# A mixture of experts in slots: slots sorted by size on the chip, short ones run over 256 columns, token numbers loaded two slots ahead

## The chip, the cores and the metric

The kernel runs on one core of a Trainium2 chip. The metric is the device time of one execution in microseconds. Engines are named as in the profile: PE is TensorE (PEld its weight loads), DVE is VectorE, ACT is ScalarE, POOL is GpSimd, SP is SyncE. A DMA is issued by the queue of one of SP, ACT or POOL; `SPq`, `ACTq` and `POOLq` are those sequencers.

## The reference

Three stages follow each other, on 4608 tokens of width 512.

```python
# attention without a softmax over pairs, 8 batches x 8 heads x 576 x 64
q_s = softmax(q, axis=-1); k_s = softmax(k, axis=2)
x = einsum('bhsd,bhde->bhse', q_s, einsum('bhsd,bhse->bhde', k_s, v))   # -> x[4608, 512]
# mixture of 8 experts, each token goes to one
logits = x @ w_gate + modality_bias[modality_id]
e_idx = argmax(logits, axis=1); gate_w = softmax(logits)[arange(N), e_idx]
for e in range(8):
    mask = e_idx == e
    out[mask] = gate_w[mask, None] * (maximum(x[mask] @ w1[e], 0) @ w2[e])   # 512 -> 1024 -> 512
# a dense layer: 512 -> 2048 -> 512, leaky relu
g = maximum(0.01 * (out @ w_in), out @ w_in);  result = g @ w_out
```

The two weight matrices of the dense layer are of type float64.

## The kernel before

Attention and router run first (`attention`), in four passes over pairs of batches. `phase_r` finds for each token its expert, its gate and its place, and scatters (token number, gate) with GpSimd's indirect DMAs into a DRAM table `region`, where each expert has 4608 rows (L384). Its tile `tg` holds the pairs to be scattered and has two buffers (L322).

`slot_tables` (L431 to L471) then works out, on the chip, how the tokens fall into slots of at most 512 rows of one expert, in the order of the experts, and leaves three integers per slot in `ti`: the expert, the first row in `region`, and the first column in `dense`. The number of slots used stands behind them. There are at most 16; slots 0 to 8 always run (`NSTATIC = 9`), slots 9 to 15 stand in nested `tc.If(ns > s)` (L692 to L699).

A slot (`slot`, L648) has two passes. Pass 1 makes 8 products of 12 matmuls over 512 columns each: a weight and an operand are each split in a high and a low part, and three of the four combinations are summed. Its result `hp` (three PSUM buffers) goes through ScalarE (`hh`, L566) and VectorE (`hl`, L567). Pass 2 makes 4 products of 24 matmuls, copied by ScalarE to `y` (L581, two buffers) and stored to `dense` by SyncE (L582). Between them stand, in the order of the code and so on each engine's queue:

- the splits of the weights for this slot's pass 2 (in pass 1) and of the next slot's pass 1 (in pass 2): `wsplit`, one ScalarE cast (L475) and one VectorE subtraction (L476) each, with the loads of weights from DRAM five pieces ahead in a ring of six buffers (L517, SyncE);
- for the next slot, `xload` at the slot's start: SyncE loads its token numbers and gates into `idt` (L541), VectorE makes integers `idi` of them (L543), GpSimd gathers the rows `xg` by four indirect DMAs (L545). After pass 1 ScalarE multiplies them by the gates (`xgate`, L551); in the second and third product of pass 2 TensorE transposes them (`xprep`, L556) and they are split into `xh` and `xl`;
- in slots 0 to 7 a conversion of the float64 weights, `f64` (L597 to L630): 16 pieces, two per slot, four steps each, of which one stands after every second product of pass 1 and one after each product of pass 2. Step 1 masks on VectorE (L610), clamps on GpSimd (L611) and loads the next piece; step 2 shifts (L615, L616); step 3 combines (L618, L619); step 4 makes four differences (L623) and splits them (`rh`, `rl`);
- in slot 8, loads for the dense layer (L748, L755).

```python
        w1 products:  for f in range(8): pass1(f); wsplit or step()
        if s + 1 < NSLOT:
            xgate(s + 1)
        for t in range(4):
            pass2(s, t, o, mid); wsplit(s + 1, 1, t); step()
```

[...] `Hidden.run` (L778) and `last_product` (L937) are the dense layer; their matmuls have 256 columns.

Of the kernel before, what the change touches and what calls it, by code (L numbers as in the profile page):

```python
# [93 lines left out]
def attention(ctx, tc, cst, a, region, xd):  # L94
# [208 lines left out]
    def phase_r(i, c0, c1):  # L303
# [122 lines left out]
SP = mybir.EngineType.SP  # L426
# [52 lines left out]
def experts(ctx, tc, cst, a, region, xd, dense, did, wops, pre):  # L479
# [17 lines left out]
    idts = [wp.tile([128, 4, 2], F32, name=f"idt{i}") for i in range(2)]  # L497
# [61 lines left out]
    def pass1(f):  # L559
# [6 lines left out]
        nc.scalar.activation(out=hh[:, f], in_=hp, func=AF.Relu)  # L566
        nc.vector.scalar_tensor_tensor(out=hl[:, f], in0=hp, scalar=0.0, in1=hh[:, f].bitcast(F32),  # L567
                                       op0=ALU.max, op1=ALU.subtract)

    def pass2(s, d, o, mid):  # L570
        yp = ps.tile([128, SLOT], F32, tag="y", name="yp")
        n = 0
        for f in range(8):
            for w, h in ((w2h, hh), (w2l, hh), (w2h, hl)):
                nc.tensor.matmul(yp, lhsT=w[:, f, 128 * d:128 * d + 128], rhs=h[:, f], start=(n == 0), stop=(n == 23))  # L575
                n += 1
# [4 lines left out]
        nc.scalar.copy(out=y, in_=yp)  # L581
        nc.sync.dma_start(out=dense[128 * d:128 * d + 128, bass.ds(o, SLOT)], in_=y)  # L582
# [14 lines left out]
    def f64(cv, name, i, w, ahead, behind):  # L597
# [13 lines left out]
        nc.gpsimd.tensor_scalar(out=t.bitcast(F32), in0=t.bitcast(F32), scalar1=CLAMP_LO, scalar2=CLAMP_HI, op0=ALU.max, op1=ALU.min)  # L611
# [36 lines left out]
    def slot(s, step=lambda: None, mid2=lambda t: None):  # L648
        if s + 1 < NSLOT:
            xload(s + 1)  # L650
        for f in range(8):
            pass1(f)
# [4 lines left out]
        if s + 1 < NSLOT:  # L657
# [3 lines left out]
                          in_=idts[s % 2].rearrange("p t c -> p (t c)"))  # L661
        for t in range(4):
# [5 lines left out]
            pass2(s, t, o, mid)  # L668
# [3 lines left out]

    loads_to(AHEAD)
# [417 lines left out]
```

## Time and profile before

| | us |
|---|---|
| runs | 1483.12, 1485.05, 1486.98 (median 1485.05) |
| profiled execution | 1477.94 |
| its span | 1476.2 |
| attention and router, to the first slot | 0 to 221 |
| ten slots | 221 to 720 |
| dense layer, first matrix | 723 to 1100 |
| dense layer, second matrix | 1105 to 1476 |
| TensorE busy | 1338.4 (91%) |
| VectorE, ScalarE, GpSimd busy | 1031.6, 600.5, 403.9 |
| mean granted clock of TensorE | 0.968 |

The profiled execution is 7 us shorter than the median of the runs. In the rows of a timeline the bracket at the end is the time that the engine was idle before the instruction, and what ended it. Matmuls are pipelined: of a run of matmuls the starts tell the pace, not the durations.

### The profile page before, as it was taken

To read this page: it belongs to the slowest core of one execution; us is meant where nothing else is said; L and a number is where in the kernel's file an instruction comes from. 1 tells how busy PE (TensorE), PEld (TensorE's weight loads), DVE (VectorE), ACT (ScalarE), POOL (GpSimd) and SP (SyncE) were. 2 spreads that over 40 slices of the span, in tenths; PEclk is the share of its full clock that TensorE was granted. 3 is DMA by queue.
4 is the path that set the end of the run, shared out by engine and by line. 5 is a ranking of instruction groups with operands and counts; after the bars stand their busy time and mean duration, and the time that the engine had idled before them with its cause. 6 is when DMAs were issued, how large, how long until landed. Compare 5 with 4: busy or idle time off the path is not lost.

```text
span 1476.2 us, 23214 instructions
## 1 busy us (share of the span) xinstructions
PE 1338.4 (91%) x9083; PEld 1229.8 (83%) x9083; DVE 1031.6 (70%) x1347; ACT 600.5 (41%) x946; POOL 403.9 (27%) x273
## 2 busy tenths in 40 slices
PE   4778718999999999989989999999989999999998
PEld 3668606777777777768889999999989999999998
DVE  5788626677767767634558777777767777777775
ACT  3566414555455545534423223332324333333332
POOL 2447532313231323011033434333331111101111
PEclk9899958999999999989999999999999999999999
DMA  9564245877787779565583333333297443443430
GB/s 374 205 241 154 103 133 171 260 242 233 249 274 232 232 246 305 194 221 179 184 346 144 121 137 136 122 133 125 103 417 295 143 143 117 135 133 118 143 115 30
DMA packets 144519, 280.05 MB, mean 190 GB/s; under 512 B 17808, under 2 KB 69520, under 8 KB 141456
## 3 DMA queue, kind: packets, MB, share of 16 engines
q1 hardware_dynamic: 125376, 218.94, 44.0%
q10 hardware_dynamic: 11472, 38.52, 6.4%
q0 software_dynamic: 7552, 21.02, 4.0%
q8 instruction: 74, 1.21, 0.3%
q14 instruction: 45, 0.37, 0.1%
HBM read 181.59 MB, written 96.85 MB: 189 GB/s over the span
## 4 chain that ended last, share of the span: by engine, by line
issue 26%; DVE 9%; PE 6%; POOL 6%; DMA 2%; ACT 1%; POOLq 0%; SPq 0%; DVEq 0%
PE hp L778 6%; POOL out L959 3%; POOL s L818 2%; DMA wi<-wid 2%; DVE ht L791 1%; DVE ht L824 1%; DVE ht L827 1%; DVE s L815 1%; DVE ht L811 1%; DVE s L813 1%; DVE x L476 1%; POOL s L819 1%; DVE xl L476 0%; ACT ht L820 0%; ACT xh L475 0%
## 5 line engine op out<-in xcount | busy, mean ns | idle before, releaser
L778 PE MATMUL hp<-xh,wi 128*128 128x256 f32 x1152 | 212.9, 281 | 3.7 <-DVE ht L827 2.3
L937 PE MATMUL yp<-wi,x 128*128 128x256 f32 x1152 | 191.5, 284 | 0.0
L778 PEld LDWEIGHTS hp<-xh,wi 128*128 128x128 f32 x1152 | 179.4, 188 | 6.3 <-DVE ht L827 3.8
L937 PE MATMUL yp<-wi,wi 128*128 128x256 f32 x1200 | 178.3, 283 | 0.3 <-DVE wi L476 0.3
L778 PE MATMUL hp<-x,wi 128*128 128x256 f32 x1296 | 166.7, 289 | 8.1 <-DMA wi<-wid 3.9
L778 PEld LDWEIGHTS hp<-x,wi 128*128 128x128 f32 x1296 | 163.1, 197 | 8.9 <-DVE ht L827 4.1
L937 PEld LDWEIGHTS yp<-wi,wi 128*128 128x128 f32 x1200 | 163.5, 192 | 0.5 <-DVE wi L476 0.5
L937 PEld LDWEIGHTS yp<-wi,x 128*128 128x128 f32 x1152 | 161.9, 192 | 0.1
L778 PE MATMUL hp<-xl,wi 128*128 128x256 f32 x576 | 160.8, 279 | 0.0
L564 PE MATMUL hp<-xh,w1h 128*128 128x512 f32 x320 | 129.7, 405 | 27.8 <-DVE hl L567 27.8
L959 POOL DMA_INDIRECT out<-yo,idx x36 | 47.4, 1317 | 314.9 <-DVE idx L953 294.3
L564 PE MATMUL hp<-xl,w1h 128*128 128x512 f32 x320 | 127.6, 399 | 0.0
L564 PE MATMUL hp<-xh,w1l 128*128 128x512 f32 x320 | 127.2, 397 | 0.0
L575 PE MATMUL yp<-hh,w2h 128*128 128x512 f32 x320 | 126.4, 395 | 0.0
L575 PE MATMUL yp<-hl,w2h 128*128 128x512 f32 x320 | 124.8, 390 | 0.0
L575 PE MATMUL yp<-hh,w2l 128*128 128x512 f32 x320 | 124.7, 390 | 0.0
L545 POOL DMA_INDIRECT xg<-xd,idi x44 | 58.3, 1325 | 237.5 <-DVE hl L567 216.8
L818 POOL TENSOR_TENSOR s<-s,s 128x512 f32<-128x512 f32 x36 | 48.3, 1343 | 226.4 <-DVE s L815 160.8
L778 PEld LDWEIGHTS hp<-xl,wi 128*128 128x128 f32 x576 | 108.0, 187 | 0.0
L791 DVE SCALAR_TENSOR_TENSOR ht<-ht 128x1024 f32<-128x1024 f32 x72 | 104.8, 1455 | 2.5
L476 DVE TENSOR_TENSOR w1l<-st,w1h 128x1024 fp32r<-128x1024 f32 x44 | 53.8, 1227 | 71.3 <-ACT w1h L475 71.3
L564 PEld LDWEIGHTS hp<-xh,w1h 128*128 128x128 f32 x320 | 61.9, 193 | 46.9 <-DVE hl L567 34.1
(202 smaller groups left out, 2629.4 us busy)
## 6 DMA issues: line engine op xcount, KB each, us to landing
st<-in_w SPq DMA_DIRECT2D x89, 512.0 KB, 5.1
hd<-ht ACTq DMA_DIRECT2D x72, 512.0 KB, 3.2
xt<-hd SPq DMA_DIRECT2D x18, 1024.0 KB, 5.4
hr<-hd SPq DMA_DIRECT2D x18, 1024.0 KB, 5.5
wi<-wid SPq DMA_DIRECT2D x28, 512.0 KB, 8.4
wi<-wod SPq DMA_DIRECT2D x6, 2048.0 KB, 13.2
v<-in_v SPq DMA_DIRECT2D x8, 1300.0 KB, 13.0
dense<-y SPq DMA_DIRECT2D x40, 256.0 KB, 3.3
```

The costliest lines, as they stand in the source:

```text
L476: nc.vector.tensor_tensor(out=lo, in0=src, in1=hi.bitcast(F32), op=ALU.subtract)
L545: nc.gpsimd.indirect_dma_start(out=xg[:, t], out_offset=None, in_=xd, in_offset=bass.IndirectOffsetOnAxis(ap=idi[:, t:t + 1], axis=0), bou ...
L564: nc.tensor.matmul(hp, lhsT=w[:, k, 128 * f:128 * f + 128], rhs=x[:, k], start=(n == 0), stop=(n == 11))
L575: nc.tensor.matmul(yp, lhsT=w[:, f, 128 * d:128 * d + 128], rhs=h[:, f], start=(n == 0), stop=(n == 23))
L778: self.nc.tensor.matmul(bank[:, g], lhsT=w[:, h, k, 128 * g:128 * g + 128], rhs=x[:, k], start=(n == 0), stop=(n == 5))
L791: V.scalar_tensor_tensor(out=c, in0=c, scalar=0.01, in1=c, op0=ALU.mult, op1=ALU.max)
L811: V.tensor_tensor(out=h[:, 0, 0], in0=bank, in1=s[1], op=ALU.add)
L813: V.tensor_tensor(out=s[6], in0=bank, in1=s[1], op=ALU.add)
L815: V.tensor_tensor(out=s[7], in0=bank, in1=s[6], op=ALU.add)
L818: G.tensor_tensor(out=s[6], in0=s[6], in1=s[5], op=ALU.add)
L937: nc.tensor.matmul(bank, lhsT=x[:, k], rhs=w[i][:, h, k], start=(c == 0), stop=(c == 23))
L959: ins = nc.gpsimd.indirect_dma_start(out=out, out_offset=bass.IndirectOffsetOnAxis(ap=idi[s % 2][:, t:t + 1], axis=0), in_=y[:, t], in_off ...
```

## The change

- **Slots sorted.** `slot_tables` counts for each expert the slots of more than 256 rows and those of up to 256, lays out all of the first kind and then all of the second (17 positions in place of 9, 16 sums in place of 8), and leaves behind the 48 integers the number of slots of the first kind (`nb`) and of all (`ns`).
- **Short slots.** In the seven dynamic blocks each slot is there twice, chosen by `tc.If(nb > s)`: as before, or with `rows=slice(0, 256)`, where matmuls, `hh`, `hl`, `y` and the store take 256 columns. The static slots stay wide.
- **Token numbers** of slot s + 2 are loaded in the middle of slot s (`idload`), into one of three buffers; those of slots 0 and 1 at the start, the first ahead of all weights.
- **Stores of `dense`** are issued by ScalarE in place of SyncE, so the column `o` is read into a register of ScalarE too.
- **The clamp** of the conversion is made by VectorE in place of GpSimd.
- `tg` has three buffers.

```diff
-            t["tg"] = sp.tile([128, NC, 2], F32, tag="tg", name="tg")
+            t["tg"] = sp.tile([128, NC, 2], F32, tag="tg", name="tg", bufs=3)
...
-    d = con.tile([128, 2, 9], F32, name="sd")
+    d = con.tile([128, 2, 17], F32, name="sd")
-    V.tensor_tensor(out=g, in0=bc(d[:, 1, 1:9], 2, 9), in1=bc(cst["k512"], 1, NE), op=ALU.is_gt)
-    V.tensor_reduce(out=d[:, 0, 1:9], in_=g, axis=AX.X, op=ALU.add)
+    V.tensor_tensor(out=g[:, 0], in0=bc(n[:, :], 2, 9), in1=bc(cst["k512"], 1, NE), op=ALU.is_gt)
+    V.scalar_tensor_tensor(out=g[:, 1], in0=bc(n[:, :], 2, 9), scalar=-256.0, in1=bc(cst["k512"], 1, NE), op0=ALU.add, op1=ALU.is_gt)
+    V.tensor_reduce(out=m, in_=g, axis=AX.X, op=ALU.add)
+    V.tensor_copy(out=d[:, 0, 1:9], in_=m[:, 1])
+    V.tensor_tensor(out=d[:, 0, 9:17], in0=m[:, 0], in1=m[:, 1], op=ALU.subtract)
...
     def reg(s, f, mx):
-        return nc.values_load(ti[0:1, 3 * s + f:3 * s + f + 1], engines=[SP], min_val=0, max_val=mx)
+        return nc.values_load(ti[0:1, 3 * s + f:3 * s + f + 1], engines=[SP] + [ACT] * (f == 2), min_val=0, max_val=mx)
...
+    def idload(s):
+        if s < NSLOT:
+            nc.sync.dma_start(out=idts[s % 3].rearrange("p t c -> p (t c)"),
+                              in_=region[bass.ds(reg(s, 1, NE * NT), SLOT), :].rearrange("(p t) c -> p (t c)", t=4))
+
     def xload(s):
-        r = reg(s, 1, NE * NT)
-        idt, idi = idts[s % 2], idis[s % 2]
-        nc.sync.dma_start(out=idt.rearrange("p t c -> p (t c)"),
-                          in_=region[bass.ds(r, SLOT), :].rearrange("(p t) c -> p (t c)", t=4))
+        idt, idi = idts[s % 3], idis[s % 2]
         nc.vector.tensor_copy(out=idi, in_=idt[:, :, 0])
...
-                nc.tensor.matmul(hp, lhsT=w[:, k, 128 * f:128 * f + 128], rhs=x[:, k], start=(n == 0), stop=(n == 11))
+                nc.tensor.matmul(hp[:, rows], lhsT=w[:, k, 128 * f:128 * f + 128], rhs=x[:, k, rows], start=(n == 0), stop=(n == 11))
...
-        nc.scalar.copy(out=y, in_=yp)
-        nc.sync.dma_start(out=dense[128 * d:128 * d + 128, bass.ds(o, SLOT)], in_=y)
+        nc.scalar.copy(out=y[:, rows], in_=yp[:, rows])
+        nc.scalar.dma_start(out=dense[128 * d:128 * d + 128, bass.ds(o, rows.stop)], in_=y[:, rows])
...
-        nc.gpsimd.tensor_scalar(out=t.bitcast(F32), in0=t.bitcast(F32), scalar1=CLAMP_LO, scalar2=CLAMP_HI, op0=ALU.max, op1=ALU.min)
+        V.tensor_scalar(out=t.bitcast(F32), in0=t.bitcast(F32), scalar1=CLAMP_LO, scalar2=CLAMP_HI, op0=ALU.max, op1=ALU.min)
...
         nc.sync.dma_start(out=did[bass.ds(o, SLOT)].rearrange("(p t) c -> p (t c)", t=4),
-                          in_=idts[s % 2].rearrange("p t c -> p (t c)"))
+                          in_=idts[s % 3].rearrange("p t c -> p (t c)"))
+        idload(s + 2)
...
+    idload(0)
+    loads_to(2)
+    idload(1)
     loads_to(AHEAD)
     xload(0)
...
-    ns = nc.values_load(ti[0:1, 3 * NSLOT:3 * NSLOT + 1], min_val=NSTATIC, max_val=NSLOT)
+    nb = nc.values_load(ti[0:1, 3 * NSLOT:3 * NSLOT + 1], min_val=0, max_val=NSLOT)
+    ns = nc.values_load(ti[0:1, 3 * NSLOT + 1:3 * NSLOT + 2], min_val=NSTATIC, max_val=NSLOT)
...
         with tc.If(ns > s):
-            slot(s)
+            before = dict(stage), list(cnt), nload[0]
+            regs.clear()
+            with tc.If(nb > s) as big:
+                slot(s)
...
+            with big.Else():
+                slot(s, rows=slice(0, SLOT // 2))
+            regs.clear()
             more(s + 1)
```

How it moves instructions shows at three places. SyncE's queue at the start of the slots, before (`st` is the ring of weights, `ti` the tables, L505 a register load):

```order
L517 DMA st_1857<-in_w 128x4x256
L517 ISA
L517 DMA st_1858<-in_w 128x4x256
L517 ISA
L517 DMA st_1859<-in_w 128x4x256
L517 ISA
L517 DMA st_1860<-in_w 128x2x512
L505 TENSOR_LOAD ti
L505 ISA x2
L541 ISA
L541 DMA idt_1862<-region 128x8
```

and now:

```order
L552 ISA
L552 DMA idt_1873<-region 128x8
L517 TENSOR_LOAD ti
L517 ISA x2
L529 ISA
L529 DMA st_1867<-in_w 128x4x256
L529 ISA
L529 DMA st_1868<-in_w 128x4x256
L517 TENSOR_LOAD ti
L517 ISA x2
L552 ISA
L552 DMA idt_1874<-region 128x8
```

The load of `idt` for slot 0 stood behind five loads of weights and now stands ahead of all of them; that of slot 1 stood after the first slot's pass 1 had begun and now follows two loads of weights.

ScalarE's queue at the end of a slot and the start of the next, before (`y` the copy of a product of pass 2, `rh` the conversion's split, `hh` the first product of pass 1):

```order
L581 COPY y_1868<-yp 128x512
L475 CAST w1h<-st_1859 128x4x256
L475 CAST xh<-tp 128x4x128 x2
L581 COPY y_1867<-yp 128x512
L475 CAST w1h<-st_1860 128x4x256
L581 COPY y_1868<-yp 128x512
L475 CAST w1h<-st_1861 128x4x256
L475 CAST rh<-r 128x1792
L566 ACTIVATE hh<-hp 128x512
```

and now:

```order
L595 COPY y_1879<-yp 128x512
L596 ISA
L596 DMA dense<-y_1879 128x512
L487 CAST w1h<-st_1869 128x4x256
L595 COPY y_1880<-yp 128x512
L596 ISA
L596 DMA dense<-y_1880 128x512
L487 CAST w1h<-st_1870 128x4x256
L487 CAST rh<-r 128x1792
L580 ACTIVATE hh<-hp 128x512
L487 CAST w2h<-st_1871 128x1024
L580 ACTIVATE hh<-hp 128x512 x2
```

Behind each copy stands the issue of its store, ahead of the next cast.

VectorE's queue in the same pass 1, before (`idi` the integers, `w2l` a split of weights):

```order
L476 TENSOR_TENSOR rl<-r,rh 128x1792
L543 CAST idi_1864<-idt_1862 128x4
L567 SCALAR_TENSOR_TENSOR hl<-hp,hh 128x512
L476 TENSOR_TENSOR w2l<-st_1856,w2h 128x1024
L567 SCALAR_TENSOR_TENSOR hl<-hp,hh 128x512
L610 TENSOR_SCALAR r<-w 128x1024
L567 SCALAR_TENSOR_TENSOR hl<-hp,hh 128x512
L476 TENSOR_TENSOR w2l<-st_1857,w2h 128x1024
L567 SCALAR_TENSOR_TENSOR hl<-hp,hh 128x512
L615 TENSOR_SCALAR w<-w 128x1024
L616 TENSOR_SCALAR r<-r 128x1024
L567 SCALAR_TENSOR_TENSOR hl<-hp,hh 128x512
```

and now:

```order
L488 TENSOR_TENSOR rl<-r,rh 128x1792
L557 CAST idi_1876<-idt_1875 128x4
L581 SCALAR_TENSOR_TENSOR hl<-hp,hh 128x512
L488 TENSOR_TENSOR w2l<-st_1867,w2h 128x1024
L581 SCALAR_TENSOR_TENSOR hl<-hp,hh 128x512
L624 TENSOR_SCALAR r<-w 128x1024
L625 TENSOR_SCALAR r<-r 128x1024
L581 SCALAR_TENSOR_TENSOR hl<-hp,hh 128x512
L488 TENSOR_TENSOR w2l<-st_1868,w2h 128x1024
L581 SCALAR_TENSOR_TENSOR hl<-hp,hh 128x512
L629 TENSOR_SCALAR w<-w 128x1024
L630 TENSOR_SCALAR r<-r 128x1024
```

The clamp (L625) stands right behind the mask; the shifts keep their places.

## Rows read from the trace of the kernel before

**Rows 1.** The page, part 1: busy time, share of the span, instructions.
```profile
PE 1338.4 (91%) x9083; PEld 1229.8 (83%) x9083; DVE 1031.6 (70%) x1347; ACT 600.5 (41%) x946; POOL 403.9 (27%) x273
```

**Rows 2.** Windows: slots 0, 1-7, 3, 8, 9; length, engines busy, clock, DMA share, GB/s.
```profile
221.20:275.90 54.70, 48.78 (x211) 39.93 (x210) 35.91 (x40) 25.43 (x32) 12.53 (x6) 0.91 0.60 189
275.90:616.20 340.30, 325.55 (x1458) 264.07 (x1457) 242.40 (x288) 168.71 (x210) 89.23 (x42) 0.99 0.78 250
373.20:422.30 49.10, 47.27 (x210) 38.77 (x209) 35.92 (x42) 24.08 (x30) 12.61 (x6) 0.97 0.77 243
616.20:674.30 58.10, 48.42 (x210) 39.62 (x209) 23.97 (x29) 23.66 (x31) 5.82 (x4) 0.91 0.66 216
674.30:720.00 45.70, 45.63 (x210) 37.60 (x208) 19.33 (x21) 21.14 (x28) 5.26 (x4) 1.00 0.47 147
```

**Rows 3.** Waits of PE (185 to 765) and ACT: total us, times, longest.
```profile
PE hp L564 <- DVE hl L567: 27.8, 15, 9.7
...
ACT y L581 <- DMA dense<-y: 28.5, 6, 5.6
```

**Rows 4.** Timeline, slot 8: start, us, engine, line, operation, [idle before, releaser].
```profile
627.28 0.36 SPq L541 DMA_DIRECT2D idt<-region  x1
...
633.53 0.17 DVE L543 CAST idi<-idt 128x4 int32<-128x4 f32 x1 [8.89 <-DMA idt<-region]
...
634.35 0.79 PE L564 MATMUL hp<-xh,w1h 128*128 128x512 f32 x1 [9.68 <-DVE hl L567]
```

**Rows 5.** Timeline of SP and DVE, from the tables to slot 0's pass 1.
```profile
196.67 2.92 SPq L517 DMA_DIRECT2D st<-in_w  x5
201.82 0.35 SPq L541 DMA_DIRECT2D idt<-region  x1
...
207.28 0.17 DVE L543 CAST idi<-idt 128x4 int32<-128x4 f32 x1 [11.64 <-DMA idt<-region]
...
226.75 1.02 SPq L594 DMA_DIRECT2D w<-in_win  x2
...
236.00 0.17 DVE L543 CAST idi<-idt 128x4 int32<-128x4 f32 x1 [8.65 <-DMA idt<-region]
```

**Rows 6.** Timeline, slot 1, pass 1 and the start of pass 2.
```profile
296.67 0.69 DVE L616 TENSOR_SCALAR r<-r 128x1024 int32<-128x1024 int32 x1 [4.59 <-POOL r L611]
...
298.02 0.50 PE L564 MATMUL hp<-xh,w1h 128*128 128x512 f32 x1 [0.39 <-DVE hl L567]
...
310.18 0.76 PE L556 MATMUL tp<-cf,xg 128*128 128x128 f32 x5 [0.28 <-ACT xg L551]
```

**Rows 7.** Timeline, end of slot 3 (SP, ACT) and start of slot 7 (PE).
```profile
411.13 3.13 SPq L594 DMA_DIRECT2D w<-in_wout  x2
...
424.32 0.59 ACT L581 COPY y<-yp 128x512 f32<-128x512 f32 x1 [5.59 <-DMA dense<-y]
...
577.48 0.50 PE L564 MATMUL hp<-xh,w1h 128*128 128x512 f32 x1 [0.81 <-DVE hl L567]
```

**Rows 8.** Window in the last product, L937 alone: length, PE and PEld busy, clock.
```profile
1200.00:1300.00 100.00, 100.00 (x837) 100.00 (x837) 1.00 0.42 132
```

**Rows 9.** Exit of the slots: timeline; L695, L690: durations ns min/median/max, first and last start.
```profile
721.79 0.55 SPq L517 DMA_DIRECT2D st<-in_w  x1
722.96 7.18 PE L778 MATMUL hp<-x,wi 128*128 128x256 f32 x36 [3.03 <-DVEq L695]
...
L695 SPq EVENT_SEMAPHORE  x9: 17/17/17, 726.8 to 727.4; - x9
...
L695 PEldq COMPARE_BRANCH  x3: 92/197/4169, 671.2 to 720.1; - x3
...
L690 PEldq TENSOR_LOAD <-ti x1: 748/748/748, 670.4 to 670.4; - x1
```

**Rows 10.** L541: time to landing; L788, stores of hd issued by ACT: duration ns.
```profile
DMA to landing us min/median/max: 3.0/3.5/7.4
...
L788 ACTq DMA_DIRECT2D hd<-ht x72: 326/326/335, 737.4 to 1111.3; - x72
```

More of the change, by code (lines that the diff above doesn't have):

```diff
@@ L446, in slot_tables @@
+    V.tensor_copy(out=d[:, 0, 1:9], in_=m[:, 1])
+    V.tensor_tensor(out=d[:, 0, 9:17], in0=m[:, 0], in1=m[:, 1], op=ALU.subtract)
+    V.tensor_tensor(out=d[:, 1, 1:9], in0=b5, in1=n, op=ALU.min)
+    V.tensor_tensor(out=d[:, 1, 9:17], in0=n, in1=d[:, 1, 1:9], op=ALU.subtract)
+    ci = con.tile([128, 2, 17], F32, name="ci")
     for f in range(2):
-        V.tensor_tensor_scan(out=ci[:, f], data0=cst["one"][:, 0:9], data1=d[:, f], initial=0.0, op0=ALU.mult, op1=ALU.add)
+        V.tensor_tensor_scan(out=ci[:, f], data0=cst["one"][:, 0:17], data1=d[:, f], initial=0.0, op0=ALU.mult, op1=ALU.add)
@@ L462, in slot_tables @@
-    pr = con.tile([128, NSLOT, 3, NE], F32, name="spr")
+    ge = con.tile([128, NSLOT, 17], F32, name="ge")
+    V.tensor_tensor(out=ge, in0=bc(sv[:, :], 2, 17), in1=bc(ci[:, 0], 1, NSLOT), op=ALU.is_ge)
+    oh = con.tile([128, NSLOT, 16], F32, name="soh")
+    V.tensor_tensor(out=oh, in0=ge[:, :, 0:16], in1=ge[:, :, 1:17], op=ALU.subtract)
+    t5 = con.tile([128, 16], F32, name="t5")
+    V.tensor_scalar(out=t5, in0=ci[:, 0, 0:16], scalar1=float(SLOT), scalar2=None, op0=ALU.mult)
+    v = con.tile([128, 3, 16], F32, name="sv3")
@@ L463, in slot_tables @@
+    V.tensor_copy(out=v[:, 0].rearrange("p (a e) -> p a e", a=2), in_=bc(cst["e"], 1, 2))
+    V.tensor_tensor(out=v[:, 1, 0:8], in0=cst["eoff"], in1=t5[:, 0:8], op=ALU.subtract)
+    V.tensor_tensor(out=v[:, 1, 8:16], in0=cst["eoff"], in1=t5[:, 8:16], op=ALU.subtract)
+    V.tensor_tensor(out=v[:, 1, 8:16], in0=v[:, 1, 8:16], in1=b5, op=ALU.add)
+    V.tensor_tensor(out=v[:, 2], in0=ci[:, 1, 0:16], in1=t5, op=ALU.subtract)
+    pr = con.tile([128, NSLOT, 3, 16], F32, name="spr")
     V.tensor_tensor(out=pr, in0=bc(oh, 2, 3), in1=bc(v, 1, NSLOT), op=ALU.mult)
@@ L467, in slot_tables @@
     V.tensor_tensor(out=r[:, :, 1:3], in0=r[:, :, 1:3], in1=bc(sv[:, :], 2, 2), op=ALU.add)
-    ti = con.tile([128, NSLOT * 3 + 1], I32, name="ti")
+    ti = con.tile([128, NSLOT * 3 + 2], I32, name="ti")
     V.tensor_copy(out=ti[:, 0:NSLOT * 3], in_=r.rearrange("p s f -> p (s f)"))
-    V.tensor_copy(out=ti[:, NSLOT * 3:NSLOT * 3 + 1], in_=ci[:, 0, 8:9])
+    V.tensor_copy(out=ti[:, NSLOT * 3:NSLOT * 3 + 2], in_=ci[:, 0, 8:17:8])
     return ti
@@ L496, in experts @@
     NST = len(ring)
-    idts = [wp.tile([128, 4, 2], F32, name=f"idt{i}") for i in range(2)]
+    idts = [wp.tile([128, 4, 2], F32, name=f"idt{i}") for i in range(3)]
     idis = [wp.tile([128, 4], I32, name=f"idi{i}") for i in range(2)]
@@ L550, in xgate @@
         for t in range(4):
-            nc.scalar.activation(out=xg[:, t], in_=xg[:, t], func=AF.Copy, scale=idts[s % 2][:, t, 1:2])
+            nc.scalar.activation(out=xg[:, t], in_=xg[:, t], func=AF.Copy, scale=idts[s % 3][:, t, 1:2])
     def xprep(k):
@@ L557, in xprep, with pass1 @@
         split(nc, *(x[:, k].rearrange("d (p t) -> d t p", t=4) for x in (xh, xl)), tp)
-    def pass1(f):
+    def pass1(f, rows):
         hp = ps.tile([128, SLOT], F32, tag="h", name="hp")
@@ L563, in pass1, with pass2 @@
             for w, x in ((w1h, xh), (w1h, xl), (w1l, xh)):
-                nc.tensor.matmul(hp, lhsT=w[:, k, 128 * f:128 * f + 128], rhs=x[:, k], start=(n == 0), stop=(n == 11))
+                nc.tensor.matmul(hp[:, rows], lhsT=w[:, k, 128 * f:128 * f + 128], rhs=x[:, k, rows], start=(n == 0), stop=(n == 11))
                 n += 1
-        nc.scalar.activation(out=hh[:, f], in_=hp, func=AF.Relu)
-        nc.vector.scalar_tensor_tensor(out=hl[:, f], in0=hp, scalar=0.0, in1=hh[:, f].bitcast(F32),
+        nc.scalar.activation(out=hh[:, f, rows], in_=hp[:, rows], func=AF.Relu)
+        nc.vector.scalar_tensor_tensor(out=hl[:, f, rows], in0=hp[:, rows], scalar=0.0, in1=hh[:, f, rows].bitcast(F32),
                                        op0=ALU.max, op1=ALU.subtract)
-    def pass2(s, d, o, mid):
+    def pass2(d, o, mid, rows):
         yp = ps.tile([128, SLOT], F32, tag="y", name="yp")
@@ L574, in pass2 @@
             for w, h in ((w2h, hh), (w2l, hh), (w2h, hl)):
-                nc.tensor.matmul(yp, lhsT=w[:, f, 128 * d:128 * d + 128], rhs=h[:, f], start=(n == 0), stop=(n == 23))
+                nc.tensor.matmul(yp[:, rows], lhsT=w[:, f, 128 * d:128 * d + 128], rhs=h[:, f, rows], start=(n == 0), stop=(n == 23))
                 n += 1
@@ L646, in conversions, with slot @@
         store()
-    def slot(s, step=lambda: None, mid2=lambda t: None):
+    def slot(s, step=lambda: None, mid2=lambda t: None, rows=slice(0, SLOT)):
         if s + 1 < NSLOT:
@@ L651, in slot @@
         for f in range(8):
-            pass1(f)
+            pass1(f, rows)
             if f % 2 == 0:
@@ L667, in mid @@
                 mid2(t)
-            pass2(s, t, o, mid)
+            pass2(t, o, mid, rows)
             if s + 1 < NSLOT:
@@ L695, in more @@
         with tc.If(ns > s):
-            slot(s)
+            before = dict(stage), list(cnt), nload[0]
+            regs.clear()
+            with tc.If(nb > s) as big:
+                slot(s)
+            stage.clear()
+            stage.update(before[0])
+            cnt[:], nload[0] = before[1:]
+            regs.clear()
+            with big.Else():
+                slot(s, rows=slice(0, SLOT // 2))
+            regs.clear()
             more(s + 1)
```

23 lines of the change are left out of this document (8 added, 15 removed).

## The prediction

> **What bounds the kernel now.** I read the page first: TensorE is busy 91% of the span [rows 1], so time can come from two places only, from work it need not do and from its pauses. The pauses were then looked for by stretch. The change touches the router's end, the ten expert slots and the start of the next product, so the windows are cut where each slot's pass 1 begins [rows 2]. Slot 9 runs without a pause: its 45.7 us are what 192 matmuls of 512 columns and 16 transposes take at the full clock. Slot 0 lasts 54.7, slots 1 to 7 together 340.3, slot 8 58.1: 9.0, 20.4 and 12.4 above that, 41.8 us of pause and of half clock. The list of waits names one owner for most: pass 1 waiting for VectorE's `hl` of three products before (`hp` has three buffers), 27.8 us [rows 3]. Why VectorE is late differs by slot.
>
> [...]
>
> Slots 1 to 7 have up to three small pauses each. VectorE waits 4.59 us for GpSimd's clamp; the eighth product then misses its `hl` by 0.39 us, and because VectorE stays behind, ScalarE gates the gathered rows late and a transpose waits 0.28 us [rows 6]. At the slot's start the conversion's split holds ScalarE and VectorE: 0.81 us in slot 7, the base case [rows 7]. Other slots have more, because the fourth block's copy `y` waits for the store of the second, which SyncE issues behind two loads of 3.13 us of issue [rows 7]; the copies do so six times [rows 3].
>
> **The change, part by part.** Token numbers two slots ahead: the waits of slots 0 and 8 go, with the half clock after them. What is late next in slot 8 is the split at its start. In slot 0 it is the first pair of loads of the second weights, issued at 226.75 [rows 5], behind which `hl` of the third product now stands: between nothing and the 5 us that the old wait covered; I take 0.7, since two more products run before it matters. The 1.3 us that the cold clock costs its first matmuls stay.
>
> Clamp on VectorE: 16 more instructions. The nearest row is the shift of the same size and engine, 0.69 us [rows 6]: one per half slot, in place of a wait of up to 4.59, so VectorE gains 3.9 us in a first pass. The 0.39 and 0.28, with the restarts behind them, go: 0.7 and 0.8 us in each of six slots, 9 us. The clamp itself is hidden behind matmuls as long as VectorE ends a first pass before the transposes of the next rows, some 8 us into pass 2; without that cover it would cost its 0.69.
>
> Stores of `dense` on ScalarE's queue: SyncE loses them, so `y` no longer waits behind loads. ScalarE gains 40 issues. Its issues of `hd` take 0.326 us [rows 10]; here each first waits for the copy just before it, so what follows starts 0.5 to 0.6 us later. In mid pass that is free. After the fourth block it stands ahead of the cast, the split and `hl`, so the base pause of 0.81 grows to 1.4, with restart 1.5 us, in slots 1 to 8. `o` is read on ScalarE once a slot, in pass 2, where it has room.
>
> Together the excess of slots 0 to 8 falls from 41.8 to 8 x 1.5 + 2.0 = 14.0: **-27.8 us**. Bounds: 8 left if the issue hides, 24 if it shifts the chain twice as far.
>
> The short slot: by the reference's inputs the experts in use hold 1019, 2289 and 1300 tokens; the tails are 507, 241 and 276, so one of ten slots has up to 256 rows, and it comes last, as slot 9. Its 192 matmuls run over 256 columns. The pace of such is 837 in 100 us in the last product [rows 8], 0.119 each, 22.9 us; with 1.8 for the transposes it is 24.8 in place of 45.7, -20.9. Against it: its block is reached by a jump over the wide one. TensorE's sequencer reads a branch ahead of its matmuls; the jump at the end took 4.169 us [rows 9], all of it while matmuls were still queued. A second register load of 0.748 now stands before the new branch: 1.5 us left open (ends 0 and 4.2). The clock may fall after such a pause, as it did in slot 3, mean 0.97 [rows 2]: 1.7 (ends 0 and 5). ScalarE has four issues more in a pass 2 of half the length: 1.6. The exit pause, 3.03 [rows 9], is `y`, a cast and a split one after the other, and gets the issue: 0.5. Sum **-15.6**, ends -19 and -8.
>
> The start: both programs can read `region` only after its last scatter, at 201.82. The numbers were there at 207.28, 5.4 us later, behind five loads of weights [rows 5]; the best landing of the eleven is 3.0 [rows 10], so the gather starts 2.4 us sooner. But the weights, issued from 196.67 before, now stand behind that wait, 5.7 us later, and share the DMA with the gather: **-1.5**, ends -3 and +3. The longer tables and the third `tg` buffer are costed at nothing: the tables were ready 5 us before that scatter.
>
> After the exit SyncE is free sooner, without `y` to wait for; it had its last load at 721.79 and issued the next weights only after 726.8 [rows 9]: **-1.0** (0 to -2.5).
>
> Sum: -27.8 - 15.6 - 1.5 - 1.0 = **-45.9**. The profiled execution took 1477.94 us, which gives 1432; the median of the runs, 1485.05, lies 7.1 above it, so I predict **1439 us**.
>
> **The rivals.**
> *Jumps eat the short slot.* [...] Chance 0.15.
>
> *The small pauses stay.* VectorE is busy 242 of the 340 us of slots 1 to 7 [rows 2], in chains with ScalarE; if it is these that are full and not GpSimd that is late, the slots keep their 20.4 us in place of 10.5, 1449 us. Against: the 4.59 us idle in the middle of such a chain. Chance 0.11.
>
> *Stores block ScalarE, slower than before.* [...] Chance 0.04.
>
> *No slot is short.* If the sort left slot 9 wide, 1455 us. Against: the counts. Chance 0.03.
>
> **How the numbers follow.** The forecast has 0.67. Its bounds reach from 1428 to 1450, and both 1449s lie in that; with the 1455 the range 1428 to 1456 leaves out the slower case and the corners where several bounds fall together. A measurement tells about 0.3%, 4.5 us, from no change: all cases but one are faster by more. Of the slower case's 0.04 a quarter is within 0.3%: 0.96, 0.01, 0.03.
>
> **What would show it.** Windows: slots 1 to 8 of 46.5 to 47.5 us, slot 9 near 28. No wait of `idi` for DMA beyond the first; no clamp on GpSimd; pass 1 waits for `hl` at the fourth product only; 40 issues on ScalarE. The forecast is wrong if slot 9 takes over 37 us, if `hh` waits for a store, or if slot 0 keeps a pause of over 3 us.

## The result, and the profile after

The changed kernel takes 1433.52 us in the median of four runs (1432.32 to 1436.11), the kernel before beside it 1484.11: a ratio of 0.9658, 95% interval 0.9638 to 0.9679, or 50.6 us less. A later comparison of the same two gave 0.9660 (0.9647 to 0.9673). The forecast was 1439 us, 1428 to 1456.

The profiled execution takes 1432.66 us (span 1430.9), 45.3 less than that of before; the sum of the prediction was 45.9. By stretch, from first matmul to first matmul:

| stretch | before, us | after, us | difference | predicted |
|---|---|---|---|---|
| start of slot 0 | 221.30 | 225.66 | +4.4 | -1.5 |
| slots 0 to 8 | 453.1 | 424.75 | -28.4 | -27.8 |
| slot 9 and exit pause | 45.5 + 3.0 | 26.0 + 6.2 | -16.3 | -15.6 |
| first matmul of the dense layer to the end of the span | 753.2 | 748.3 | -5.0 | -1.0 |

The page of the changed kernel, part 1 (before: [rows 1]):

```profile
PE 1310.8 (92%) x9083; PEld 1215.1 (85%) x9083; DVE 1036.2 (72%) x1371; ACT 601.7 (42%) x946; POOL 342.7 (24%) x257
```

TensorE is busy 28 us less with as many matmuls, GpSimd 61 us less. Its windows, cut as before ([rows 2]): slot 0, slots 1 to 7, slot 8, slot 9, and the first matrix of the dense layer (length, busy time of PE, PEld, DVE, ACT, POOL, granted clock, DMA share, GB/s):

```profile
225.66:274.52 48.86, 47.87 (x210) 39.21 (x209) 35.56 (x42) 25.71 (x32) 4.83 (x4) 0.95 0.74 240
274.52:602.45 327.93, 319.78 (x1457) 263.28 (x1456) 247.63 (x302) 171.48 (x210) 35.80 (x28) 1.00 0.79 255
...
602.45:650.41 47.96, 45.85 (x209) 37.42 (x207) 24.18 (x29) 24.61 (x32) 5.77 (x4) 1.00 0.81 276
650.41:676.44 26.03, 25.47 (x208) 24.83 (x208) 16.57 (x21) 18.19 (x27) 4.72 (x4) 1.00 0.64 208
682.60:1054.70 372.10, 365.68 (x3024) 362.36 (x3024) 279.21 (x345) 116.83 (x205) 137.62 (x105) 0.99 0.46 179
```

Slots 1 to 7 now take 46.85 us each, all alike; slot 8 loses its half clock (before, a granted clock of 0.50 from 634.35 to 639.00 us), slot 0 keeps it only in its first 5 us (a granted clock of 0.50 to 0.61 there, 1.00 behind). The waits of PE from slot 0 to the end of the first matrix:

```profile
PE hp L578 <- DVE hl L581: 10.3, 9, 1.2
PE hp L807 <- DVEq L714: 6.2, 1, 6.2
...
PE hp L807 <- DMA wi<-wid: 2.4, 3, 1.4
...
PE hp L578 <- ACT y L595: 0.9, 1, 0.9
```

The wait for `hl` (27.8 us, 15 times, longest 9.7 in [rows 3]) is 10.3 in nine pieces: 1.16 in each of slots 1 to 8, at the fourth product, and 0.99 in slot 0, at the sixth. The exit's wait has doubled. The last line is the entry of the short slot; its 0.9 us lie in the row of slots 0 to 8 of the table.

### The profile page after: what moved, and what is told of

Read it like the earlier page. It is cut to its first block, busy times and chain, and to the rows that moved or that the text cites. A ratio compares the mean times of both kernels' runs of the same rounds, so it can differ in the third digit from the quotient of the medians.

```text
span 1430.9 us, 23212 instructions
## 1 busy us (share of the span) xinstructions
PE 1310.8 (92%) x9083; PEld 1215.1 (85%) x9083; DVE 1036.2 (72%) x1371; ACT 601.7 (42%) x946; POOL 342.7 (24%) x257
## 4 chain that ended last, share of the span: by engine, by line
issue 26%; DVE 9%; PE 8%; POOL 6%; DMA 2%; ACT 1%; POOLq 0%; SPq 0%; DVEq 0%; ACTq 0%
PE hp L807 8%; POOL out L988 3%; POOL s L847 2%; DMA wi<-wid 2%; DVE ht L820 1%; DVE ht L856 1%; DVE ht L853 1%; DVE s L844 1%; DVE ht L840 1%; DVE x L488 1%; DVE s L842 1%; POOL s L848 1%; DMA hd<-ht 1%; DVE xl L488 0%; DVE xt L795 0%
## 5 line engine op out<-in xcount | busy, mean ns | idle before, releaser
L807 PEld LDWEIGHTS hp<-x,wi 128*128 128x128 f32 x1296 | 160.2, 194 | 8.2 <-ACTq L714 6.4
L578 PE MATMUL hp<-xh,w1h 128*128 128x512 f32 (+1 forms) x320 | 123.4, 386 | 11.2 <-DVE hl L581 10.3
L589 PE MATMUL yp<-hh,w2h 128*128 128x512 f32 (+1 forms) x320 | 122.9, 384 | 0.0
L578 PE MATMUL hp<-xh,w1l 128*128 128x512 f32 (+1 forms) x320 | 121.9, 381 | 0.0
L578 PE MATMUL hp<-xl,w1h 128*128 128x512 f32 (+1 forms) x320 | 121.9, 381 | 0.0
L589 PE MATMUL yp<-hl,w2h 128*128 128x512 f32 (+1 forms) x320 | 121.5, 380 | 0.0
L589 PE MATMUL yp<-hh,w2l 128*128 128x512 f32 (+1 forms) x320 | 121.4, 379 | 0.0
L847 POOL TENSOR_TENSOR s<-s,s 128x512 f32<-128x512 f32 x36 | 48.3, 1341 | 208.7 <-DVE s L844 160.8
L849 ACT ACTIVATE ht<-s 128x512 f32<-128x512 f32 x36 | 22.8, 633 | 149.7 <-POOL s L848 145.1
```

The costliest lines, as they stand in the source:

```text
L578: nc.tensor.matmul(hp[:, rows], lhsT=w[:, k, 128 * f:128 * f + 128], rhs=x[:, k, rows], start=(n == 0), stop=(n == 11))
L589: nc.tensor.matmul(yp[:, rows], lhsT=w[:, f, 128 * d:128 * d + 128], rhs=h[:, f, rows], start=(n == 0), stop=(n == 23))
L807: self.nc.tensor.matmul(bank[:, g], lhsT=w[:, h, k, 128 * g:128 * g + 128], rhs=x[:, k], start=(n == 0), stop=(n == 5))
L847: G.tensor_tensor(out=s[6], in0=s[6], in1=s[5], op=ALU.add)
L849: nc.scalar.activation(out=h[:, 1, 1], in_=s[5], func=AF.Relu)
```

## The experiments

Eleven kernels ran, in three groups; each has its ratio to the kernel before on the same chip. The kernel before had medians of 1478.8, 1484.1, 1487.6 and 1489.4 us in the four comparisons, so ratios, not times, are compared across groups.

**The kernel before again.**

> The kernel before, unchanged, for a second profile of it. What is asked: the first slot began 4.4 us later after the change (225.66 against 221.30), with the last scatter into region 8.4 us later (204.76 against 196.41). Theory 1, the attention's own length differs from one execution to the next: in this second profile the last scatter lies anywhere from 196 to 206, several us from 196.41, and the slots keep their 498.6 us. Theory 2, something in the change (the third buffer of tg, the longer tables) delays the scatters: here it lies at 196.4 within 1.5 us.

1487.94 us. The slots repeat (452.7 for 0 to 8, against 453.1). The last scatter starts at 202.66, not 196.41, and the first slot at 231.88. Timeline of SyncE, VectorE and PE at the start:

```profile
205.15 0.15 DVE L470 CAST ti<-ci 128x1 int32<-128x1 f32 x1
206.33 2.84 SPq L517 DMA_DIRECT2D st<-in_w  x5
210.04 0.61 SPq L541 DMA_DIRECT2D idt<-region  x1
...
217.81 0.17 DVE L543 CAST idi<-idt 128x4 int32<-128x4 f32 x1 [12.52 <-DMA idt<-region]
...
231.88 0.78 PE L564 MATMUL hp<-xh,w1h 128*128 128x512 f32 x1
```

Theory 1 holds: the attention's length differs by several us with the change out of play. And here not the scatter but the tables (`ti`) are last, 2.6 us behind it. Five loads of weights then go first, and the numbers arrive 12.5 us after the tables.

**Token numbers alone.** The edit is that of `idload` and its four calls:

```diff
-        nc.sync.dma_start(out=idt.rearrange("p t c -> p (t c)"),
...
+        idload(s + 2)
...
+    idload(0)
+    loads_to(2)
+    idload(1)
```

> The kernel before with the token numbers loaded two slots ahead (and those of slots 0 and 1 at the start), nothing else. Theory 1, the sum of the prediction: slot 0 falls from 54.7 to 47 to 49, slot 8 from 58.1 to 46.5 to 47.5, the other slots stay as they are, together -18 us (-16 to -21), 1466 us. Theory 2, the waits lean on each other: in slot 0 the load of the second weights' first pair takes its place and half of the pause stays (slot 0 at 51 or more), together -12 us or less.

Ratio 0.9863 (0.9833 to 0.9894). Windows of slot 0, slots 1 to 7, slot 8:

```profile
226.32:274.63 48.31, 47.07 (x210) 38.49 (x209) 36.28 (x40) 25.34 (x32) 12.01 (x6) 0.98 0.67 214
274.63:614.82 340.19, 325.98 (x1457) 264.03 (x1456) 243.25 (x287) 169.02 (x210) 88.67 (x42) 0.99 0.77 250
614.82:661.21 46.39, 45.69 (x210) 37.61 (x208) 23.76 (x28) 23.71 (x31) 5.82 (x4) 1.00 0.83 274
```

Theory 1: slot 0 at 48.3, slot 8 at 46.4, the seven between them unchanged to 0.1 us (340.3 before). Slots 0 to 8 give 17.8 us against the second profile of before, and slot 0 starts 19.9 us behind the tables in place of 26.6.

**The clamp alone.**

```diff
-        nc.gpsimd.tensor_scalar(out=t.bitcast(F32), in0=t.bitcast(F32), scalar1=CLAMP_LO, scalar2=CLAMP_HI, op0=ALU.max, op1=ALU.min)
+        V.tensor_scalar(out=t.bitcast(F32), in0=t.bitcast(F32), scalar1=CLAMP_LO, scalar2=CLAMP_HI, op0=ALU.max, op1=ALU.min)
```

> The kernel before with the clamp of the conversion on VectorE, nothing else. Theory 1, the sum of the prediction: the pauses at the eighth product and at the transposes go, 1.5 us in each of six to eight slots, -9 us (-7 to -12); slots of 46.9 to 48. Theory 2, the chains of VectorE and ScalarE are full and GpSimd is not what is late: the wait moves to the slot's start, -3 us or less, and slots 1 to 7 keep 48.5 us in the mean.

Ratio 0.9929 (0.9904 to 0.9954). The window of slots 1 to 7, and the one pause that is left in a slot, from the timeline of slot 1:

```profile
292.25:616.48 324.23, 319.32 (x1457) 263.35 (x1456) 248.21 (x301) 170.03 (x210) 35.82 (x28) 1.00 0.80 260
...
301.28 0.50 PE L564 MATMUL hp<-xh,w1h 128*128 128x512 f32 x1 [0.70 <-DVE hl L567]
```

324.2 in place of 340.3: 16.1 us, well over the 9 of theory 1, with every slot at 46.3. Not only the pauses at the eighth product and the transposes are gone. Those beyond 0.70 at the slot's start are gone too, and ScalarE's list of waits has no wait of `y` for a store any more (28.5 us in [rows 3]), though SyncE still issues the stores. The copies were late because the conversion was: its stores and its next load went out late and held SyncE. In slots 1 to 6 of the kernel before SyncE issued the second store of `y` 7.9 to 8.8 us before the slot's end; here it does so 9.0 to 10.0 before it. Why GpSimd was late shows in the durations of the clamp, before (POOL) and after (DVE):

```profile
L611 POOL TENSOR_SCALAR r<-r x16: 3623/3650/4188, 243.2 to 604.6; 128x1024 f32<-128x1024 f32 x16
```

```profile
L625 DVE TENSOR_SCALAR r<-r x16: 694/695/697, 241.3 to 589.9; 128x1024 f32<-128x1024 f32 x16
```

VectorE paid 0.695 us in place of a wait for 3.65. The time fell by less than the slots. In this profile the tables came 5.4 us behind the last scatter and slot 0 began at 237.0, 5 us later than in the second profile of before; the clamp has no part in that stretch, and whether the other runs were late there too isn't on record.

**The stores alone.**

```diff
-        nc.sync.dma_start(out=dense[128 * d:128 * d + 128, bass.ds(o, SLOT)], in_=y)
+        nc.scalar.dma_start(out=dense[128 * d:128 * d + 128, bass.ds(o, SLOT)], in_=y)
```

> The kernel before with the stores of dense issued by ScalarE, nothing else. Theory 1, the sum of the prediction: no copy waits for a store any more (28.5 us of waits of ScalarE before), which evens the slots 1 to 7 out at about 48.5 us, and each store's issue lengthens the pause at the slot's start to 1.4 us; together -1 us (-4 to +3). Theory 2, the stores are the larger part: without waits of y the slots of 49 us and more fall to 47, -7 us or more. Theory 3, a store holds ScalarE: hh waits for stores, +4 us or more.

Ratio 0.9982 (0.9964 to 0.9999). Slots 1 to 7, and the pause at the fourth product of slot 1:

```profile
293.27:631.69 338.42, 324.69 (x1457) 262.83 (x1456) 241.85 (x288) 170.39 (x210) 88.73 (x42) 1.00 0.78 248
...
302.76 0.50 PE L564 MATMUL hp<-xh,w1h 128*128 128x512 f32 x1 [1.16 <-DVE hl L567]
```

Theory 1: the slots even out at 48.35, and the issue lengthens the pause to 1.16, where the clamp alone left 0.70. No `hh` waits for a store.

**The stores back on SyncE, all else as changed.**

```diff
-        nc.scalar.dma_start(out=dense[128 * d:128 * d + 128, bass.ds(o, rows.stop)], in_=y[:, rows])
+        nc.sync.dma_start(out=dense[128 * d:128 * d + 128, bass.ds(o, rows.stop)], in_=y[:, rows])
```

> The changed kernel with the stores of dense back on SyncE's queue. Theory 1, the runs of single parts added up: the clamp alone took slots 1 to 7 to 46.3 us, stores on ScalarE lengthened the pause at the slot's start from 0.70 to 1.16; so this kernel has slots of 46.3 to 46.4, nine times -0.5, and a slightly shorter exit: -4 to -6 us against the changed kernel, 1428 to 1430. Theory 2, with the short slot or with idt two ahead the copies y again wait for stores behind SyncE's loads: slots of 46.8 or more, no gain or a loss.

Ratio 0.9663 (0.9636 to 0.9690): the same as the changed kernel. The slots did what theory 1 said, the time did not. Slots 1 to 7, and TensorE's branch into the short slot:

```profile
282.33:607.06 324.73, 319.85 (x1457) 263.27 (x1456) 248.36 (x301) 169.88 (x210) 35.81 (x28) 1.00 0.81 260
...
L717 PEldq COMPARE_BRANCH  x1: 6227/6227/6227, 650.8 to 650.8; - x1
```

The 3.2 us that slots 1 to 7 gain are lost elsewhere: the entry of the short slot takes 2.5 more (3.5 us of pause behind a branch of 6.23 us), and exit and dense layer together 2.5 more (4.7 + 752.3, against 6.2 + 748.3). Slot 0 takes 2.7 more as well, but it took as much with the weights first and the stores on ScalarE, so that isn't the stores' doing. In the slots it is a loss that ScalarE issues the stores. Of the six runs two took 1433.9 and 1434.4 us and four 1440.1 to 1444.4, and the profile (1442.4) is of one of the four. Whether the longer entry and the longer rest belong to the stores or to this execution stays open; the ratio sees no difference.

**Two buffers of `tg`, all else as changed.**

```diff
-            t["tg"] = sp.tile([128, NC, 2], F32, tag="tg", name="tg", bufs=3)
+            t["tg"] = sp.tile([128, NC, 2], F32, tag="tg", name="tg")
```

> The changed kernel with two buffers of tg, as before. Theory 1, the third buffer ends ScalarE's wait for the scatters (5.6 to 7.2 us at its last copy of tg in the kernel before) that makes the tables late: the tables are ready 2.5 to 5 us after the last scatter in place of 0.3 before it, token numbers are read later, and the start of slot 0 lies 24 to 27 us behind the last scatter in place of 20.9: +2 to +5 us. Theory 2, the scatters alone set the start, the tables are covered: 20.9 within 1 us, no change in the time.

Ratio 0.9672 (0.9652 to 0.9692). The tables are ready 6.1 us after the last scatter and slot 0 starts 25.7 behind it. But with three buffers on the same chip the tables came 4.2 to 4.7 us after it (three kernels), not before it as in the profile of the change. So the third buffer moves the tables by some 1.4 to 1.9 us at most, and the interval of the ratio holds no change as well: unsettled in size.

**The weights first, all else as changed.**

```diff
-    idload(0)
-    loads_to(2)
-    idload(1)
     loads_to(AHEAD)
+    idload(0)
+    idload(1)
```

> The changed kernel with the token numbers of slots 0 and 1 loaded behind the first five loads of weights, as they stood for slot 0 before. Theory 1: what the start gained it gained here, since behind five loads the numbers take 5.4 to 7.8 us to land in place of 1 to 1.6 after their issue, and are issued 3 us later where the tables are what is late: start of slot 0 at 24 to 28 us behind the last scatter in place of 20.9, +3 to +6 us. Theory 2, the prediction's bound: the gather gains 2.4 and loses as much by sharing the DMA with the weights: no change beyond 1.5 us.

Ratio 0.9702 (0.9678 to 0.9726), some 6.5 us above the changed kernel by the ratios. VectorE, SyncE and PE at the start:

```profile
209.92 0.16 DVE L482 CAST ti<-ci 128x2 int32<-128x2 f32 x1
211.11 2.84 SPq L529 DMA_DIRECT2D st<-in_w  x5
214.82 1.50 SPq L552 DMA_DIRECT2D idt<-region  x2
...
221.91 0.17 DVE L557 CAST idi<-idt 128x4 int32<-128x4 f32 x1 [11.84 <-DMA idt<-region]
...
235.91 0.78 PE L578 MATMUL hp<-xh,w1h 128*128 128x512 f32 x1
```

Theory 1. From tables to slot 0 it is 25.8 us here, and 26.1 to 27.0 in the three kernels of the first group that load weights first; with the numbers first and the tables late it is 19.6 to 19.9 (four kernels). The numbers come 9 us sooner (2.7 to 2.9 us after the tables in place of 11.8 to 12.9), and the gather, now beside the weights, gives 2.8 of it back (16.8 to 17.2 us from `idi` to the first matmul in place of 14.0 to 14.2). In the 9.1 us behind `idi` the DMA engines are busy to 0.56 here, and to 0.99 in the next run, where the numbers go first.

**Only the dynamic block of slot 9.**

```diff
-        if s == NSLOT:
+        if s == NSTATIC + 1:
             return
```

> The changed kernel with the dynamic block of slot 9 only; blocks 10 to 15, which these inputs don't run, are left out. Theory 1: the exit's 6.20 us (3.03 before) are the jump over six blocks that now hold two slots each; ScalarE's next instruction came 4.80 us after its branch (2.54 before), and TensorE waited for it. Without them ScalarE goes on within 0.5 us, the exit falls to 3.0 to 3.6 us, -2.5 to -3.5 us. Theory 2, the exit is the copy, the store's issue, a cast and a split one after the other and the split is what is late: exit at 5.5 us or more, within 1 us of the changed kernel.

Ratio 0.9632 (0.9613 to 0.9650). The changed kernel's exit first: VectorE's last split in the slots, its branch and its next instruction, and PE's first matmul behind it (two windows of line L714, and the timelines):

```profile
678.39 1.23 DVE L488 TENSOR_TENSOR w1l<-st,w1h 128x1024 fp32r<-128x1024 f32 x1 [1.65 <-ACT w1h L487]
...
L714 DVEq COMPARE_BRANCH  x1: 56/56/56, 678.4 to 678.4; - x1
...
L714 DVEq EVENT_SEMAPHORE  x1: 21/21/21, 682.5 to 682.5; - x1
...
682.63 6.68 PE L807 MATMUL hp<-x,wi 128*128 128x256 f32 x36 [6.20 <-DVEq L714]
```

VectorE shows nothing for 4.05 us behind its branch, 2.9 of them after its split has ended, and TensorE starts 0.1 after it. ScalarE is silent for 4.8 us behind its own branch, to 682.2, but TensorE doesn't wait for it, as the expectation took it to: in the run with two buffers of `tg` ScalarE comes back at 690.1, VectorE at 689.6, and TensorE starts at 689.70. In the kernel before VectorE went on as soon as its split ended, at 722.8:

```profile
721.58 1.23 DVE L476 TENSOR_TENSOR w1l<-st,w1h 128x1024 fp32r<-128x1024 f32 x1 [4.21 <-ACT w1h L475]
...
L695 DVEq COMPARE_BRANCH  x1: 67/67/67, 721.6 to 721.6; - x1
...
L695 DVEq EVENT_SEMAPHORE  x1: 21/21/21, 722.8 to 722.8; - x1
```

Without the blocks to jump over, the pause is gone altogether, by more than theory 1 said. The waits of PE there in this experiment:

```profile
PE hp L807 <- ACT x L487: 2.4, 1, 2.4
PE hp L807 <- DVE ht L820: 1.7, 1, 1.7
PE hp L807 <- DMA wi<-wid: 0.8, 1, 0.8
PE hp L807 <- DVE x L488: 0.8, 1, 0.8
```

The dense layer's first product runs at once, and then waits for its operands: from slot 9 to the end it is 779.8 us, against 780.5 in the changed kernel and 778.8 in its second profile. The pause is a jump's, but it covers waits that come due without it. The ratio is 0.0026 below the changed kernel's, some 4 us, with intervals that overlap; in the profile slot 9 to the end gives none of it, so where it would lie stays open.

**The changed kernel again.** No edit.

> The changed kernel, unchanged, for a second profile of it beside the next two. Theory 1: its slots, exit and dense layer repeat within 2 us; the start of slot 0 lies 18 to 20 us behind the tables, as in the runs with the token numbers first (18.6 to 20.1), where it is 26.0 to 27.2 with the weights first. Theory 2, the 20.9 us between last scatter and first slot belong to the third buffer of tg: they repeat within 1 us.

Ratio 0.9660 (0.9647 to 0.9673). Slots 0 to 8 take 424.9, slot 9 25.0, the exit 6.2, the rest 747.6. On this chip the tables are ready before the last scatter; slot 0 starts 21.9 behind them and 21.0 behind the scatter, which is what is late here. So theory 2's number repeats and theory 1's misses by 2; but theory 2's cause doesn't stand, since three other kernels with three buffers had 24 us and more. The start goes by whichever of tables and scatter is later.

**The last split ahead of the last copy.** In the fourth product of pass 2 `wsplit` and `step` move to its middle:

```diff
                 mid2(t)
+                if t == 3:
+                    if s + 1 < NSLOT:
+                        wsplit(s + 1, 1, t)
+                    step()
             pass2(t, o, mid, rows)
-            if s + 1 < NSLOT:
-                wsplit(s + 1, 1, t)
-            step()
+            if t < 3:
...
```

> The changed kernel with the last split of weights of a slot and the fourth step of the conversion placed in the middle of the fourth product of pass 2, ahead of the copy y and its store on ScalarE's queue. Theory 1: the pause of 1.16 us at each slot's start is the chain copy, issue, cast, split, differences, split, which now starts 1.8 us sooner; the pause goes in eight or nine slots, slots 1 to 7 at 45.7 to 45.9 us, -8 to -10 us. Theory 2, VectorE is full at this place and its own work sets the pause: slots of 46.6 or more, -2 us or less.

Ratio 0.9591 (0.9577 to 0.9604): 1417.51 us, where the changed kernel beside it took 1427.48. Windows of slots 1 to 7 and of slot 9, and the waits of PE from there:

```profile
269.45:587.06 317.61, 317.61 (x1457) 263.82 (x1456) 247.55 (x302) 171.66 (x210) 35.83 (x28) 1.00 0.82 264
...
633.54:658.58 25.04, 25.04 (x208) 24.84 (x208) 15.41 (x19) 18.24 (x27) 4.00 (x4) 1.00 0.72 215
```

```profile
PE hp L812 <- DMA wi<-wid: 4.1, 1, 4.1
PE hp L812 <- DVEq L719: 3.3, 1, 3.3
```

Theory 1: in slots 1 to 7 TensorE doesn't pause at all, 45.37 us each. The exit shortens by 2.9 too; the 3.3 us that are left of it are the jumps (TensorE's own branch ends at 661.2, VectorE comes back at 661.7, 3.0 behind its branch). But the dense layer then waits 4.1 for its weights, and takes 6 more from its first matmul to the end. This kernel beats both.

**Without the short path.** The seven blocks hold one wide slot each:

```diff
-            with tc.If(nb > s) as big:
-                slot(s)
...
-            with big.Else():
-                slot(s, rows=slice(0, SLOT // 2))
+            slot(s)
```

> The changed kernel without the short path: each dynamic block holds one slot of 512 columns. Theory 1, the prediction's term of 15.6 us for the short slot: slot 9 takes 45.5 to 46 in place of 26.0, the exit falls from 6.2 to 3.0 to 3.6 since the jump is over half as much; +15 to +18 us. Theory 2, the short slot's gain is given back at its exit and after it: +10 us or less.

Ratio 0.9764 (0.9751 to 0.9777): 1444.13, 16.7 above the changed kernel beside it. Slot 9; then PE's wait at the exit, VectorE's last split there, and the next instruction behind its branch of VectorE and of ScalarE:

```profile
645.40:690.93 45.53, 45.53 (x209) 37.51 (x207) 19.50 (x21) 21.61 (x28) 3.99 (x4) 1.00 0.43 142
```

```profile
PE hp L799 <- DVEq L714: 3.5, 1, 3.5
...
693.10 1.23 DVE L488 TENSOR_TENSOR w1l<-st,w1h 128x1024 fp32r<-128x1024 f32 x1 [4.26 <-ACT w1h L487]
...
L714 DVEq EVENT_SEMAPHORE  x1: 21/21/21, 694.4 to 694.4; - x1
...
L714 ACTq EVENT_SEMAPHORE  x2: 17/17/17, 695.1 to 695.2; - x2
```

Theory 1 in the numbers, but the exit of 3.5 isn't a shorter jump that shows. It is the old chain with the store's issue in it: VectorE goes on as its split ends, TensorE starts 0.1 behind it (694.48), and ScalarE comes back only after that. The short slot is worth 16.7 us by the medians, with its exit counted. (From slot 9 to the end the two profiles differ by 19.1.)

## Why the prediction was right, and where it was not

*Token numbers two slots ahead.* Right in mechanism and size: alone they give 17.8 us in slots 0 and 8, and leave the rest as it was. In slot 0 a smaller pause takes its place, as was said (0.99 and 1.9 us in the two profiles of the changed kernel, 1.2 to 3.2 in the experiments, for 0.7 predicted). It is the pause that was named, behind the first pair of loads of the float64 weights:

```profile
240.54 0.69 DVE L624 TENSOR_SCALAR r<-w 128x1024 int32<-128x1024 int32 x1 [5.71 <-DMA w<-in_win]
```

The clock in slot 8 is 1.00. Before, behind the wait for the token numbers [rows 4], TensorE's matmuls took 0.79 us and then 0.63 each, those of slot 9 0.39.

*The clamp.* Right in mechanism, mis-sized: 9 us were predicted for the slots, 16.1 were measured. The step that failed is the one that gave the late copies `y` to SyncE's loads and so to the stores' move. They were a further effect of the late clamp: with it the pauses beyond 0.70 at the slot's start went, 5.1 us in all in slots 1 to 7, while the stores alone gave 1.9 there.

*The stores.* The issue does stand ahead of the cast and lengthens the chain at the slot's start, from 0.70 to 1.16 us, 0.46 a slot where 0.6 was taken (0.81 to 1.4). Its gain in the slots is nil, since the clamp had already removed the waits of `y`. That the sum of slots 0 to 8 came out to 0.6 us is owed to its form: it was made from what would be left, 14.0 us, and not from the gains of single edits. Those would have been split wrongly. It is owed to luck as well, since errors in what is left nearly cancel: slots 1 to 7 keep 1.15 us each for 1.5, slot 8 keeps 2.3 for 1.5 (the short slot's entry is in it), and slot 0 3.2 for 2.0, of which the clock of its first matmuls costs 2.2 for 1.3.

*The short slot.* 15.6 predicted, 16.3 by the two profiles, 16.7 by the run without it. Inside the term two errors nearly cancel. The entry costs 0.94 us for 1.5, there is no loss of clock (1.00, for 1.7) and none that shows to ScalarE's issues (for 1.6): slot 9 with its entry takes 27.0 in place of 29.6. The exit, in turn, grew by 3.2 for 0.5 (of which the dense layer gave most back, below). The old exit was read rightly, as copy, cast and split in a row, and the issue is worth the 0.5: with a wide slot 9 the exit takes 3.03 without it, and 3.5 with it (the stores alone, and the run without the short path). The step that failed is that the jump behind the exit was put at nothing. At the old exit VectorE is back 1.2 us after its branch, and its own split covers that; over six blocks that hold two slots each it takes 4.05, and 2.9 of them outlast the split. The exit is where the rival "jumps eat the short slot" (0.15, one of the two 1449s) came true. That VectorE and ScalarE lose some 4 us at the entry too was the author's estimate; no run shows it, and in the changed kernel VectorE's next instruction stands 0.2 us behind its branch there and ScalarE's 0.4. At the entry TensorE's jump over one wide block took 3.67 us, nearly all of it while matmuls were queued:

```profile
L717 PEldq COMPARE_BRANCH  x1: 3667/3667/3667, 646.7 to 646.7; - x1
...
650.41 0.39 PE L578 MATMUL hp<-xh,w1h 128*128 128x256 f32 x1 [0.94 <-ACT y L595]
```

The profile names `y`; the branch ends at 650.4, 0.3 us after it, and in the run where the branch took 6.23 us the pause was 3.5. What the time of a jump goes into, no run shows. Measured are TensorE's branch over one wide block (3.67 and 3.51 us in the two profiles of the changed kernel, 6.23 with the stores on SyncE), the exit's pause, which is gone with no blocks behind it, and, between 676 and 683 us of the changed kernel's trace, five transfers of instructions, four of them inside VectorE's silence.

*The start.* Mis-sized: 1.5 us predicted; where the tables are late, it is 6 to 7 us less from the tables to slot 0. The step that failed is "both programs can read `region` only after its last scatter", with the tables 5 us earlier. That held in the one profiled execution, whose tables were ready at 195.6 and whose last scatter was issued at 196.41, with the load of the numbers held until 201.82. In the second profile of before the tables are what is late, so five loads of weights stand ahead of the numbers for the whole of their time. There the longer tables, which were costed at nothing, take something back: VectorE works 5.9 to 6.2 us on them in place of 3.9 to 4.2. The profile of before was thus too good at the start. This hides the gain in the pair of profiles (+4.4, with the attention 8 us longer); the medians differ by 50.6 us, the profiles by 45.3. That the forecast from the median missed by 5.5 us for this fits these numbers, but isn't shown, since only one execution of each of the two was profiled there.

*Behind the exit.* 1.0 predicted, 5.0 measured, but this and the longer exit are one thing: what the jump holds up is waited for less afterwards. Exit and dense layer together take 756.2 us before and 754.5 after, -1.7 for a predicted -0.5. In the eleven experiments the sum lies between 752.4 and 757.0, however the exit fell out: 6.2 + 747.6 in the second profile of the change, 3.3 + 753.6 with the last split moved. So the step that failed is to price exit and the loads behind it as two terms that add up.

The small pauses went (that rival is out by the clamp's run), no store held ScalarE (its waits at `hh` in the slots are 87.1 us for products and 3.1 with no releaser named; that a store has to wait there, the slower case's 0.04, no run shows), and slot 9 was short.

## What to carry to other kernels

When several edits meet in one chain, predict what is left when all are made, and don't price each edit by the wait that bears its name: the late copies here were named for a store and caused by a clamp that took GpSimd 3.65 us. Before taking a stretch's critical wait from one profile, look whether another candidate lies within a few us of it there, as the tables and the last scatter did (0.8 us from the one's end to the other's issue), and price the edit for either order. A jump over code cost microseconds here on each of three engines (at the exit 4.97 us on TensorE, 4.05 on VectorE, 4.8 on ScalarE), and was hidden where the engine still had work of its own. So read the first instruction of each engine behind its branch, see when that engine's last work ended, and check which of the engines the waiting one needs.

## What was not expected

- The same clamp takes GpSimd 3.65 us and VectorE 0.695.
- VectorE is held up in the tables, by up to 1.9 us at a time, around GpSimd's last scatters. From the run with the clamp alone, where the last scatter's record runs from 205.49 to 206.46:

```profile
207.01 0.17 DVE L460 TENSOR_TENSOR sv<-cf,t 128x8 f32<-128x8 f32 x1 [1.65 <-remote]
...
209.14 0.56 DVE L463 TENSOR_TENSOR spr<-soh,sv 128x384 f32<-128x384 f32 x1 [1.88 <-remote]
```

  These stalls go with the order at the start. VectorE idles 0.4 us within the tables in the profile of before and in the three of the last group, 1.1 in the first profile of the change, and there the tables are ready before the last scatter is issued; in the other eight profiles it idles 3.5 to 6.7, and the tables are ready after it. What holds VectorE there, no run shows; the second stall above begins after the last scatter's record has ended.
- With the numbers first the gather takes 2.8 us longer from `idi` to the first matmul, beside the weights in the DMA engines.
